# Seven PSUM banks in one tile, handed out one by one, in a fused attention and feed-forward kernel

## The chip, the cores and the metric

One Trainium2 chip, of which the kernel uses one core. The metric is the device time of one execution in microseconds. Five engines run their own instruction streams: TensorE (PE) multiplies matrices into PSUM, ScalarE (ACT) does exponentials and tanh, VectorE (DVE) does elementwise work, GpSimd (POOL) only sets constants at the start here, SyncE (SP) issues most DMAs. PSUM is used here as eight banks of 128 partitions x 512 float32 columns.

## The reference

The output mixes an attention block and a feed-forward block, token by token, with a sigmoid gate. There are 2048 tokens of 512 features, 32 heads of 16 features, and 1792 hidden features; everything is bf16.

```python
    def _A_ref(x, wqkv, wo):
        ...
        qkv = (lambda x, *d: x.transpose(*d))((x @ wqkv).reshape(B, S, 3, H, Dh), 2, 0, 3, 1, 4)
        q, k, v = qkv[0], qkv[1], qkv[2]
        scores = jnp.einsum("bhqd,bhkd->bhqk", q, k) * (Dh ** -0.5)
        p = _softmax(scores, axis=-1)
        o = jnp.einsum("bhqk,bhkd->bhqd", p, v)
        return (lambda x, *d: x.transpose(*d))(o, 0, 2, 1, 3).reshape(B, S, D) @ wo

    def _B_ref(x, w_gate, w_up, w_down):
        g = _silu(x @ w_gate)
        u = x @ w_up
        return (g * u) @ w_down

    x = A_x
    g = _sigmoid((x * gate_w).sum(-1, keepdims=True))
    a = _A_ref(x, A_wqkv, A_wo)
    b = _B_ref(x, B_w_gate, B_w_up, B_w_down)
    return g * a + (1 - g) * b
```

## The kernel before

**Tiling.** The attention is cut into 32 units: 4 blocks of 512 queries times 8 groups of 4 heads. Each unit walks over 16 key tiles of 128 keys. For one key tile of one unit there are 4 score blocks, one for each head, of 128 keys x 512 queries: one PSUM bank each. The 2048 score blocks are all computed by TensorE (`score`), with a contraction over 32 rows, so that up to four of them run side by side in the array.

**Two ways to an exponential.** Most score blocks go to ScalarE: `emit_pair` takes a PSUM tile of two banks from the pool `ps_s` (two such tiles in turn), puts two score blocks into it and lets ScalarE write the exponentials of 1024 columns to a tile `e_t` in SBUF, one of `EB` = 10. The other key tiles go to VectorE: `emit_d` puts one score block into a single bank, VectorE reads it with a multiply and an add into 16-bit integers (`c_t<-d_t` in the profile), and further VectorE instructions in SBUF (`copy`, or `bits` and `product`) make an exponential out of the bits. `v_unit`, `v_take` and `quad` choose which key tiles go that way and in which of the two forms. An `emit_d` rides along with the scores of a pair.

**PV.** `pv` multiplies the exponentials with the values and sums into one bank of its own (`ps_o`, tile `o_ps`), four column tiles of 32 at a time.

**Side work.** The projections (`kp`, `qp`, `vp`), the gated feed-forward (`gu`, `dps`) and the output projection (`ops`) are cut into pieces of four matmuls of 32 columns by `columns`. Each chain of pieces takes one bank from three single-bank pools `ps_m0` to `ps_m2` (`m_tile`), and VectorE or ScalarE reads the bank at its end (`m_free`). A `Pacer` releases chains by deadlines.

**The order.** Every instruction of an engine goes through a helper (lines 164, 167 and 176) that ties it to the one before on that engine, so the order in which the program is written is the order in which each engine runs. What decides it is a planner in Python, which keeps a running time for TensorE, ScalarE and VectorE (`plan.pe`, `plan.act`, `plan.dve`) and when each bank comes free (`banks`, and `s_end` for the two score tiles). The main loop fills the time until the next score tile is free with PV, side pieces or a short wait, and then emits the pair. Exponentials are collected in `exps` and written into the program by `flush_act` once the planner's time has reached them; VectorE's work is written by `fill_dve`. Which instruction waits for which is worked out by the framework from the tiles that they read and write.

```python
        def exp():
            act(out=e_t[:], in_=s_t[:], func=ACT.Exp, scale=inv_sqrt_dh)
            plan.act = max(plan.act, ready) + ACT_US
            s_end[i] = plan.act + SLOT
```

The start (transposing the input, the first keys, queries and values) and the end (the last rows of the output) are written out by hand; they use the same pools.

## Time and profile before

| what | value |
|---|---|
| median of 3 runs | 780.14 us (778.90 to 780.59) |
| the profiled execution: span from first to last instruction | 777.2 us |
| the profiled execution's own time | 777.15 us of span; what the runs add around it is 2.99 us to the median |
| ScalarE busy | 762.2 us in 861 instructions |
| TensorE busy | 741.1 us in 9412 matmuls |
| VectorE busy | 722.4 us in 1171 instructions |
| exponentials of two banks | 792, 743.8 us together, 1198 ns each |
| reads of single banks `d_t` by VectorE | 464 |
| mean granted TensorE clock | 0.999 of full speed |

The profile is of one execution. "Busy" is the time in which an engine had at least one instruction in it; since ScalarE overlaps instructions that follow each other, 792 instructions of 1198 ns take 743.8 us. Matmul ends are modelled. In the groups, the part after the bar is the busy time in us, the mean of one in ns, and the engine's idle time just before them with what ended it. A line of the waits reads: who waited, for whom, total us, how often, the longest.

### The profile page before, as it was taken

To read this page: it belongs to the slowest core of one execution; us is meant where nothing else is said; L and a number is where in the kernel's file an instruction comes from. 1 tells how busy PE (TensorE), PEld (TensorE's weight loads), DVE (VectorE), ACT (ScalarE), POOL (GpSimd) and SP (SyncE) were. 2 spreads that over 40 slices of the span, in tenths; PEclk is the share of its full clock that TensorE was granted. 3 is DMA by queue.
4 is the path that set the end of the run, shared out by engine and by line. 5 is a ranking of instruction groups with operands and counts; after the bars stand their busy time and mean duration, and the time that the engine had idled before them with its cause. 6 is when DMAs were issued, how large, how long until landed. Compare 5 with 4: busy or idle time off the path is not lost.

```text
span 777.2 us, 22732 instructions
## 1 busy us (share of the span) xinstructions
PE 741.1 (95%) x9412; PEld 237.2 (31%) x9413; DVE 722.4 (93%) x1171; ACT 762.2 (98%) x861; POOL 10.6 (1%) x25
## 2 busy tenths in 40 slices
PE   8999999999999999999999999999999989999997
PEld 3333333323332232333222233323322323333232
DVE  7799999999999999989999999999999899899992
ACT  6999999999999999999999999999999999999996
POOL 5000000000000000000000000000000000000000
PEclk9999999999999999999999999999999999999999
DMA  8002304144210112221100230311000322100001
GB/s 190 2 2 48 76 12 80 28 115 88 63 26 12 26 44 61 60 46 31 34 19 18 49 83 19 76 35 40 17 24 14 85 54 57 30 19 12 14 29 35
DMA packets 91022, 34.42 MB, mean 44 GB/s; under 512 B 75488, under 2 KB 90472, under 8 KB 90920
## 3 DMA queue, kind: packets, MB, share of 16 engines
q1 hardware_dynamic: 89192, 32.66, 17.5%
q8 instruction: 73, 1.20, 0.7%
q10 hardware_dynamic: 1728, 0.33, 0.2%
q14 instruction: 29, 0.24, 0.1%
HBM read 21.55 MB, written 2.35 MB: 31 GB/s over the span
## 4 chain that ended last, share of the span: by engine, by line
ACT 44%; PE 40%; issue 8%; DVE 7%; DMA 0%; ACTq 0%; DVEq 0%
ACT e_t L167 41%; PE s_t L164 15%; PE o_ps L164 10%; PE gu L164 7%; DVE c_t L176 5%; PE ops L164 4%; ACT th L167 4%; PE qp L164 1%; PE kp L164 1%; DVE kaug L176 1%; PE dps L164 1%; PE warm L164 1%; DVE mt L176 1%; DVE gs L176 0%; DMA wu<-in_B_w_up_dram 0%
## 5 line engine op out<-in xcount | busy, mean ns | idle before, releaser
L167 ACT ACTIVATE e_t<-s_t 128x1024 bf16<-128x1024 f32 x792 | 743.8, 1198 | 1.9 <-PE s_t L164 1.9
L176 DVE TENSOR_SCALAR c_t<-d_t 128x512 uint16<-128x512 f32 x404 | 268.7, 685 | 18.1 <-PE d_t L164 17.6
L164 PE MATMUL s_t<-qx,kaug 32*128 32x512 bf16 (+1 forms) x1248 | 243.5, 381 | 17.6 <-ACT e_t L167 14.5
L164 PEld LDWEIGHTS <-kaug 32*128 32x128 bf16 (+1 forms) x2048 | 103.8, 91 | 320.2 <-issue 314.8
L164 PE MATMUL o_ps<-e_t,vaug 128*32 128x512 bf16 (+3 forms) x1828 | 164.2, 356 | 0.0
L164 PE MATMUL d_t<-qx,kaug 32*128 32x512 bf16 x384 | 133.5, 384 | 0.0
L176 DVE TENSOR_SCALAR c_t<-c_t 128x2048 uint16<-128x2048 uint16 x187 | 125.7, 687 | 1.1
L164 PEld LDWEIGHTS <-vaug 128*32 128x32 bf16 x3416 | 74.9, 95 | 109.2 <-issue 89.3
L164 PE MATMUL o_ps<-c_t,vaug 128*32 128x512 bf16 (+3 forms) x1316 | 104.3, 334 | 1.0 <-DVE osb L176 0.5
L176 DVE TENSOR_TENSOR c_t<-c_t 128x2048 bf16<-128x2048 bf16 x63 | 76.7, 1218 | 0.0
L164 PE MATMUL gu<-xT,wg 128*32 128x512 bf16 x896 | 74.1, 384 | 0.0
L164 PE MATMUL gu<-xT,wu 128*32 128x512 bf16 x896 | 68.9, 382 | 0.0
L164 PE MATMUL ops<-wd_t,mt 128*32 128x512 bf16 x672 | 57.8, 382 | 0.0
L164 PE MATMUL s_t<-q,kaug 64*128 64x512 bf16 (+1 forms) x200 | 39.0, 382 | 7.5 <-ACT e_t L167 7.1
L167 ACT ACTIVATE th<-gu 128x512 bf16<-128x512 f32 x56 | 43.4, 775 | 0.0
L176 DVE SCALAR_TENSOR_TENSOR gs<-th,gu 128x512 bf16<-128x512 bf16 x56 | 38.2, 683 | 5.4 <-ACT th L167 5.2
L176 DVE SCALAR_TENSOR_TENSOR mt<-gs,gu 128x512 bf16<-128x512 bf16 x56 | 38.2, 682 | 1.5 <-PE gu L164 0.5
L176 DVE TENSOR_SCALAR kaug<-d_t 128x512 uint16<-128x512 f32 x56 | 37.4, 684 | 1.1 <-PE d_t L164 1.1
L164 PEld LDWEIGHTS <-mt 128*32 128x32 bf16 (+1 forms) x1037 | 23.6, 95 | 24.6 <-issue 21.3
L176 DVE TENSOR_SCALAR kaug<-c_t 128x2048 uint16<-128x2048 uint16 x39 | 26.8, 686 | 0.5 <-PE o_ps L164 0.4
L164 PEld LDWEIGHTS <-wu 128*32 128x32 bf16 x896 | 19.3, 95 | 22.8 <-issue 15.4
L164 PEld LDWEIGHTS <-wg 128*32 128x32 bf16 x896 | 16.2, 94 | 25.9 <-issue 25.4
(141 smaller groups left out, 436.3 us busy)
## 6 DMA issues: line engine op xcount, KB each, us to landing
wg<-in_B_w_gate_dram SPq DMA_DIRECT2D x56, 128.0 KB
wu<-in_B_w_up_dram SPq DMA_DIRECT2D x56, 128.0 KB
on<-osb SPq DMA_DIRECT2D x120, 16.0 KB
rb<-rr SPq DMA_DIRECT2D x15, 128.0 KB
wd_t<-in_B_w_down_dram SPq DMA_DIRECT2D x7, 256.0 KB
qx<-qst SPq DMA_DIRECT2D x96, 16.0 KB
qx<-aq SPq DMA_DIRECT2D x96, 16.0 KB
out_dram<-o_t SPq DMA_DIRECT2D x12, 128.0 KB
```

What stands on the lines that cost most here:

```text
L164: return ordered(nc.tensor.matmul(*args, **kw))
L167: ordered(nc.scalar.activation(*args, **kw))
L176: return lambda *a, **kw: ordered(f(*a, **kw))
```

## The change

The pools `ps_s` and `ps_m0` to `ps_m2` go. One tile `psum` of seven banks takes their place, and each bank is handed out by itself, to score blocks and side work alike (`take`, `single`, `runs`). `emit_group` replaces `emit_pair`: it takes one, two or three banks with a constant step (`choose`), which need not be neighbours, and one exponential reads them all in one instruction. The blocks are counted in quarters of a key tile, so that a group of three may straddle two key tiles. The ten tiles `e_t` become one tile `e_all` of 22 blocks. The planner's fixed delays are replaced by completion times: an exponential ends at its start plus 0.064 (or 0.167 after a wait) plus 0.4265 for each block, and so on.

```diff
-    etp = ctx.enter_context(tc.tile_pool(name="etp", bufs=EB))
+    etp = ctx.enter_context(tc.tile_pool(name="etp", bufs=1))
...
-    ps_s = ctx.enter_context(tc.tile_pool(name="ps_s", bufs=2, space=bass.MemoryType.PSUM))
+    ps_b = ctx.enter_context(tc.tile_pool(name="ps_b", bufs=1, space=bass.MemoryType.PSUM))
     ps_o = ctx.enter_context(tc.tile_pool(name="ps_o", bufs=1, space=bass.MemoryType.PSUM))
-    ps_m = [ctx.enter_context(tc.tile_pool(name=f"ps_m{i}", bufs=1, space=bass.MemoryType.PSUM)) for i in range(3)]
+    psum = ps_b.tile([P, NP, QBW], F32, name="psum")
...
-    banks = [0.0] * 3
-    held = [None] * 3
+    banks = [0.0] * NP
+    held = [None] * NP
+
+    FLIP, UNIT_US = 0.105, 0.217
+    TO_ACT, ACT_FIX, ACT_COL, ACT_IN = 0.485, 0.064, 0.4265, 0.167
+    ACT_PE, DVE_PE, PE_DVE, ACT_DVE = 0.055, 0.08, 0.24, 0.06
...
     def m_tile(name):
         while m_ready() is None:
             stuck()
-        i = min((i for i in range(3) if banks[i] is not None), key=lambda i: banks[i])
+        i = single()
         plan.pe = max(plan.pe, banks[i])
+        return take(i)
+
+    def take(i):
         banks[i] = None
-        held[i] = ps_m[i].tile([P, QBW], F32, tag=f"m{i}", name=name)
+        held[i] = psum[:, i, :]
         return held[i]
...
+    def runs(w, now):
+
+        ok = [b is not None and b <= now for b in banks]
+        return [(i, s) for s in range(1, NP) for i in range(NP - (w - 1) * s) if all(ok[i + k * s] for k in range(w))]
+
+    def single():
+
+        first = min(b for b in banks if b is not None)
+        now = max(first, plan.pe)
+        open_ = [i for i in range(NP) if banks[i] is not None and banks[i] <= now]
+        ...
+        return max(open_, key=lambda i: (left(i), -banks[i]))
...
-    def emit_pair(bs, ride=0):
-        i = pairs[0] % 2
-        plan.pe = max(plan.pe + (FLIP if plan.mode != "R" else 0.0), s_end[i])
+    e_all = etp.tile([P, NE, QBW], BF16, name="e_all")
+    def choose():
+
+        late = max(plan.pe, horizon() - LATEST)
+        ...
+        for w in range(most, 0, -1):
+            if best is not None and w < 2:
+                break
+            r = runs(w, late) or (runs(w, 1e9) if best is None and w <= 2 else [])
+            if not r:
+                continue
+            s = min(([i + k * d for k in range(w)] for i, d in r), key=spread)
+            ...
+            key = (n, bool(fit), w) if dry else (n > 0 or not want, w)
+            if best is None or key > best[0]:
+                best = key, s, n, got
+        return best and best[1:]
...
+    def emit_group(s, ride, rel):
+        nonlocal quarter, at_, begun
+        w = len(s)
+        bs = next_banks(w)
+        ...
+        k0, step = s[0], s[1] - s[0] if w > 1 else 1
+        s_t = psum[:, k0:k0 + (w - 1) * step + 1:step, :]
+        ...
         for k, b in enumerate(bs):
-            score(s_t[:, k * QBW:(k + 1) * QBW], b, 32 if ride else 64)
-            e_of[b] = e_t[:, k * QBW:(k + 1) * QBW]
-        for k in ride:
+            score(psum[:, s[k], :], b, 32 if riders or w != 2 else 64)
+            e_of[b] = e_all[:, e0 + k, :]
+            e_slot[b] = e0 + k
+        for k in riders:
             emit_d(k)
-        spend("R", 1)
+        spend("R", 2 if extra else 1)
         flush_act()
-        ready = plan.pe + 0.27
+        ready = start + TO_ACT
 
         def exp():
-            act(out=e_t[:], in_=s_t[:], func=ACT.Exp, scale=inv_sqrt_dh)
-            plan.act = max(plan.act, ready) + ACT_US
-            s_end[i] = plan.act + SLOT
+            act(out=e_all[:, e0:e0 + w, :], in_=s_t, func=ACT.Exp, scale=inv_sqrt_dh)
+            plan.act = max(plan.act + ACT_FIX, ready + ACT_IN) + ACT_COL * w
+            for i in s:
+                banks[i] = plan.act + ACT_PE
...
-    kp0 = ps_s.tile([P, 2 * QBW], F32, tag="s", name="kp0")
-    qp0 = m_tile("qp0")
+    def pair_at(i):
+        banks[i] = banks[i + 1] = None
+        return psum[:, i:i + 2, :].rearrange("p b q -> p (b q)")
+
+    kp0 = pair_at(0)
+    qp0 = take(4)
...
-        room = s_end[pairs[0] % 2] - plan.pe
+        s, ride, rel = s
+        room = max(rel, horizon() - LATEST) - FLIP - plan.pe
...
-        emit_pair([4 * n + 2 * half, 4 * n + 2 * half + 1], want_d())
-        half ^= 1
-        begun = 0
-        at_ += not half
-        forward()
+        emit_group(s, ride, rel)
```

More of the change, by code (lines that the diff above doesn't have):

```diff
@@ L116 @@
     EB = 10
+    NE = 22
+    NP = 7
     NY = 3
@@ L128 @@
     MUL_US = 1.135
+    LATEST = 0.64
     TINY = 1e-37
@@ L131 @@
     QLEAD = 24
-    SPARE = 0.5
+    SPARE = 0.3
     const = ctx.enter_context(tc.tile_pool(name="const", bufs=1))
@@ L305, in spend @@
         work_at.append((plan.pe, mms))
-        plan.pe = max(plan.pe + (FLIP if mode != plan.mode else 0.0), ready) + (0.226 if mode == "F" else 0.217) * mms
+        plan.pe = max(plan.pe + (FLIP if mode != plan.mode else 0.0), ready) + (0.226 if mode == "F" else UNIT_US) * mms
         plan.mode = mode
@@ L313, in later @@
             c.owed += 1
-        ready = plan.pe + 0.25 if ready is None else ready
+        ready = plan.pe + PE_DVE if ready is None else ready
         owed.insert(sum(o[0] <= ready for o in owed), (ready, cost, f, c, key))
@@ L358, in m_free, with left @@
         i = [h is ps for h in held].index(True)
-        banks[i], held[i] = t + 0.2, None
+        banks[i], held[i] = t + DVE_PE, None
+    def runs(w, now):
[5 more added lines that the diff above has]
+        open_ = [i for i in range(NP) if banks[i] is not None and banks[i] <= now]
+        def left(i):
+            keep, banks[i] = banks[i], None
+            n = len(runs(3, 1e9))
+            banks[i] = keep
+            return n
+        return max(open_, key=lambda i: (left(i), -banks[i]))
     def emit_piece(c):
@@ L604, in end @@
             vec.reciprocal(odds[:, :], ge[:, :])
-        later(0.5, end, plan.act + 0.2)
+        later(0.5, end, plan.act + ACT_DVE)
     def turn_odds():
@@ L623 @@
     FS = [(qb, fc) for qb in ORDER for fc in range(FC)]
-    w_gate, w_up, gs_of = {}, {}, {}
+    w_gate, w_up, gs_of, gs_at = {}, {}, {}, {}
     def w_load(i, gate):
@@ L642, in gate @@
             th = work.tile([P, QBW], BF16, tag="th", name="th")
-            flush_act(plan.pe + 0.4)
+            ready = plan.pe + TO_ACT - UNIT_US
+            flush_act(ready + 0.05)
             act(out=th[:], in_=gp[:, :], func=ACT.Tanh, scale=0.5)
-            plan.act = max(plan.act, plan.pe + 0.25) + 0.48
+            plan.act = max(plan.act + ACT_FIX, ready + ACT_IN) + ACT_COL
             def f():
@@ L651, in f @@
                 gs_of[i] = gs
-            later(0.6, f, plan.act + 0.25)
+            gs_at[i] = plan.act + ACT_DVE
+            later(0.62, f, gs_at[i])
         cs = slice(FS[i][0] * QBW, (FS[i][0] + 1) * QBW)
         return [columns(DC, "gu", lambda dc, w=w: w[i][:, dc, :], lambda dc: xT[:, dc, cs], end)
-                for w, end in ((w_gate, gate), (w_up, lambda p: later(0.6, lambda: gated(p))))]
+                for w, end in ((w_gate, gate), (w_up, lambda p: later(0.6, lambda: gated(p), max(plan.pe + PE_DVE, gs_at[i]))))]
     scaled = set()
@@ L690, in score @@
            tile_position=(r.start, 0))
-    FLIP = 0.107
-    SLOT = 0.28
-    s_end = [0.0, 0.0]
     e_end = {}
-    e_left = {}
-    pairs = [0]
-    def emit_pair(bs, ride=0):
-        i = pairs[0] % 2
-        plan.pe = max(plan.pe + (FLIP if plan.mode != "R" else 0.0), s_end[i])
-        plan.mode = "R"
-        ride = d_slots(1 - bs[0] % 4 // 2)[:ride]
-        s_t = ps_s.tile([P, 2 * QBW], F32, tag="s", name="s_t")
-        e_t = etp.tile([P, 2 * QBW], BF16, tag="e", name="e_t")
+    e_all = etp.tile([P, NE, QBW], BF16, name="e_all")
@@ new lines, with e_run, dur, horizon @@
+    e_slot = {}
+    e_next = [0]
+    def e_run(w):
+        used = set(e_slot.values())
+        for k in range(NE):
+            i = (e_next[0] + k) % NE
+            if i + w <= NE and not any(j in used for j in range(i, i + w)):
+                return i
+        return None
+    def dur(w):
+        return ACT_FIX + ACT_COL * w
+    def horizon():
+        return max(plan.act + dur(exps[-1][2]), exps[-1][0] + ACT_IN + ACT_COL * exps[-1][2]) if exps else plan.act
+    def fitting(w):
+        heads = {HEADS[b % 4] for b in next_banks(w)}
+        return [k for k in d_slots() if HEADS[k] not in heads]
@@ new lines, in choose, with spread @@
+    def choose():
+        late = max(plan.pe, horizon() - LATEST)
+        want = wants()
+        dry = thirst() < 1.5
+        side_b = int(side_bank())
+        most = min(3, 4 * (hi[au] - at_) - quarter) if au == UNITS - 1 else 3
+        def spread(s):
+            keep = [banks[i] for i in s]
+            for i in s:
+                banks[i] = None
+            left = len(runs(3, 1e9)) + len(runs(2, 1e9))
+            for i, t in zip(s, keep):
+                banks[i] = t
+            return max(max(keep), plan.pe), -left
+        best = None
+        for w in range(most, 0, -1):
[5 more added lines that the diff above has]
+            s = min(([i + k * d for k in range(w)] for i, d in r), key=spread)
+            rel = max(banks[i] for i in s)
+            others = sorted(b for i, b in enumerate(banks) if b is not None and i not in s and b <= max(late, rel))
+            n = max(0, min(want, len(others) - side_b, 3 - len(d_wait)))
+            fit = len(fitting(w)) if n else 0
+            n = min(n, fit) if fit or not dry else min(n, 1)
+            got = max(rel, others[n - 1]) if n else rel
+            key = (n, bool(fit), w) if dry else (n > 0 or not want, w)
+            if best is None or key > best[0]:
+                best = key, s, n, got
+        return best and best[1:]
@@ new lines, in next_banks @@
+    def next_banks(w):
+        r, a, t, q = [], au, at_, quarter
+        while len(r) < w and a < UNITS:
+            r.append(4 * (a * KT + t) + q)
+            q += 1
+            if q == 4:
+                q, t = 0, t + 1
+                while a < UNITS and t == hi[a]:
+                    a, t = a + 1, 0
+        return r
+    def emit_group(s, ride, rel):
+        nonlocal quarter, at_, begun
+        w = len(s)
+        bs = next_banks(w)
+        begun = 1
+        start = max(plan.pe + (FLIP if plan.mode != "R" else 0.0), rel)
+        spare[0] = min(spare[0] + max(0.0, horizon() - LATEST - start - 0.1), 1.5)
+        plan.pe = start
+        plan.mode = "R"
+        for i in s:
+            banks[i] = None
+        e0 = e_run(w)
+        e_next[0] = e0 + w
+        k0, step = s[0], s[1] - s[0] if w > 1 else 1
+        s_t = psum[:, k0:k0 + (w - 1) * step + 1:step, :]
+        riders = fitting(w)[:ride] if ride else []
+        extra = ride and not riders
+        if extra:
+            riders = d_slots()[:1]
@@ L715, in exp @@
         def exp():
-            act(out=e_t[:], in_=s_t[:], func=ACT.Exp, scale=inv_sqrt_dh)
-            plan.act = max(plan.act, ready) + ACT_US
-            s_end[i] = plan.act + SLOT
+            act(out=e_all[:, e0:e0 + w, :], in_=s_t, func=ACT.Exp, scale=inv_sqrt_dh)
+            plan.act = max(plan.act + ACT_FIX, ready + ACT_IN) + ACT_COL * w
+            for i in s:
+                banks[i] = plan.act + ACT_PE
             for b in bs:
-                e_end[b] = plan.act + 0.27
-        exps.append((ready, exp))
@@ L722, in emit_pair @@
-        for b in bs:
-            e_left[b] = pairs[0]
-        pairs[0] += 1
+                e_end[b] = plan.act + ACT_PE
+        exps.append((ready, exp, w))
+        for _ in bs:
+            quarter += 1
+            if quarter == 4:
+                quarter = 0
+                at_ += 1
+                begun = 0
+                forward()
+                begun = int(quarter > 0)
+            else:
+                begun = 1
+        begun = int(quarter > 0)
     exps = []
-    ACT_US = 0.905
@@ L729, in flush_act @@
     def flush_act(before=None):
-        while exps and (before is None or max(plan.act, exps[0][0]) <= before):
+        while exps and (before is None or max(plan.act - 0.33, exps[0][0]) <= before):
             exps.pop(0)[1]()
@@ L735, with d_slots @@
     y_live = [0]
-    def d_slots(half=None):
-        left = vcur["left"] if vcur else range(NV)
-        return [k for k in left if half is None or k // 2 == half]
+    def d_slots():
+        return list(vcur["left"] if vcur else range(NV))
     users = {}
@@ L797, in first @@
                     vops.append((0.6, lambda k=k: copy(n, k, h, y), ("y", n) if k == 1 else None, n, True))
-        d_wait.append((plan.pe + 0.5, first, n))
+        d_wait.append((plan.pe + UNIT_US + PE_DVE, first, n))
     waiting = {}
@@ L805, in ready @@
         copies[n, k] = (c.bitcast(BF16), h)
-        vready.append((plan.dve + 0.3, n, k))
+        vready.append((plan.dve + DVE_PE, n, k))
     def copy(n, k, i, y):
@@ L812, in copy @@
         if k == 3:
-            drop(i, plan.dve + 0.2)
+            drop(i, plan.dve + 0.05)
             y_live[0] -= 1
@@ L828, in product @@
         ready(n, 1, i, c)
-        drop(h, plan.dve + 0.2)
+        drop(h, plan.dve + 0.05)
         y_live[0] -= 1
@@ L884, in take_part @@
         vec.tensor_copy(out=o_part, in_=o_of[0][:, :])
-        o_end[0] = plan.dve + 0.2
+        o_end[0] = plan.dve + DVE_PE
         part_done.append(0)
@@ L927, in pv @@
                 e_of.pop(b)
-                e_left.pop(b, None)
+                e_slot.pop(b)
         pvs[un] += 1
         if un == 0 and pvs[0] == KT // 2:
-            later(0.6, take_part, plan.pe + 0.47)
+            later(0.6, take_part, plan.pe + UNIT_US + PE_DVE)
         spend("C", share, 0.0 if k is not None else max(e_end.pop(b, 0.0) for b in range(4 * n, 4 * n + 4)))
@@ L1038, in tail_ready @@
         assert here_done and len(scaled) == TQ
-        al = ps_s.tile([P, 2 * QBW], F32, tag="s", name="al")
-        a_ps.append(al)
+        a_ps.append(m_tile("al"))
     def tail(n):
@@ L1095 @@
     keep_warm(12)
-    tp = ps_s.tile([P, 2 * QBW], F32, tag="s", name="tp")
+    tp = pair_at(2)
     turn(DC - 1, [tp[:, 0:QBW], tp[:, QBW:2 * QBW]])
@@ L1099 @@
     pad(0)
-    tps = [m_tile("tp") for _ in range(2)]
+    tps = [take(i) for i in (5, 6)]
     turn(DC - 2, tps)
@@ L1127 @@
     plan.dve = plan.pe + 3.9
+    for i in range(4):
+        banks[i] = 0.0
     pace = Pacer()
@@ L1267 @@
     pace.add(last_pieces(), SLOTS - KT // 2, SLOTS, downs, cond=ripe)
-    au = at_ = half = begun = 0
+    au = at_ = quarter = begun = 0
     vu = 0
@@ L1313, in f @@
             post(un)
-            o_end[0] = plan.dve + 0.2
+            o_end[0] = plan.dve + DVE_PE
             finish(un)
@@ L1427 @@
     LEAD, LAST = 8.0, 6.0
-    TILE_US = 1.87
+    TILE_US = 1.82
     def forward():
         nonlocal au, at_
-        while au < UNITS and not half and not begun and at_ == hi[au]:
+        while au < UNITS and not begun and at_ == hi[au]:
             au, at_ = au + 1, 0
@@ L1442, in v_unit @@
                 return None
-            left = hi[vu] - (at_ + max(half, begun) if vu == au else 0)
+            left = hi[vu] - (at_ + begun if vu == au else 0)
             if vu >= au and left > 0 and (vu or hi[0] > KT // 2):
@@ L1461, in quad, with wants, thirst, side_bank @@
         if spare[0] > SPARE:
-            spare[0] = 0.0
+            spare[0] -= SPARE
             return False
         return True
-    def want_d():
-        if not vcur and v_unit() is None:
-            return 0
+    def wants():
+        if len(d_wait) >= 3 or not vcur and v_unit() is None:
+            return 0
+        return 2 if thirst() < 1.5 else 1
+    def thirst():
+        return 0.6 * len(d_wait) + sum(v[0] for v in vops) + plan.dve - plan.pe
+    def side_bank():
         c = pick()
-        one = c is not None and c.pieces[c.i][2] and (pace.credit > 0 or c.deadline <= plan.slot + 4)
-        open_ = sum(b is not None and b <= plan.pe for b in banks)
-        if not d_wait and len(vops) < 2:
-            one = False
-        return max(0, min(2, open_ - int(one), 3 - len(d_wait)))
+        return bool(c is not None and c.pieces[c.i][2] and (pace.credit > 0 or c.deadline <= plan.slot + 4)
+                and (d_wait or len(vops) >= 2))
     while au < UNITS:
@@ L1481 @@
         flush_act(plan.pe)
-        back = pairs[0] - min(e_left.values(), default=pairs[0])
-        if back >= EB - 1:
+        back = len(e_slot) // 2
+        if back >= EB or e_run(3) is None:
             next_pv()
             continue
-        room = s_end[pairs[0] % 2] - plan.pe
+        s = choose()
+        if s is None:
+            flush_act()
+            s = choose()
+            if s is None:
+                stuck()
+                continue
+        s, ride, rel = s
+        room = max(rel, horizon() - LATEST) - FLIP - plan.pe
         if room > 0.02:
@@ L1489 @@
             switch = 0.0 if plan.mode == "C" else FLIP
-            fits = int((room + SLACK - switch) / 0.216)
+            fits = int((room + SLACK - switch) / UNIT_US)
             c = side(room + SLACK)
@@ L1515 @@
                 spend("C", 1)
-                spare[0] += 0.22
                 continue
-            if room > 0.15:
+            if rel > plan.pe + 0.15:
                 plan.pe += 0.1
-                spare[0] += 0.1
                 continue
-        n = au * KT + at_
-        begun = 1
-        emit_pair([4 * n + 2 * half, 4 * n + 2 * half + 1], want_d())
-        half ^= 1
-        begun = 0
-        at_ += not half
-        forward()
+        emit_group(s, ride, rel)
     flush_act()
@@ L1568 @@
     tail(2)
-    rps = ps_s.tile([P, 2 * QBW], F32, tag="s", name="rps")
+    rps = m_tile("rps")
     spread_rows(rps, rt)
```

## The prediction

> **What bounds the kernel now.** I read the page's engine totals first, then the chain that ended last, then the costliest groups, the list of waits, and two stretches of the timeline for the price of single steps.

> ```profile
> PE 741.1 (95%) x9412; PEld 237.2 (31%) x9413; DVE 722.4 (93%) x1171; ACT 762.2 (98%) x861; POOL 10.6 (1%) x25
> ACT 44%; PE 40%; issue 8%; DVE 7%; DMA 0%; ACTq 0%; DVEq 0%
> L167 ACT ACTIVATE e_t<-s_t 128x1024 bf16<-128x1024 f32 x792 | 743.8, 1198 | 1.9 <-PE s_t L164 1.9
> L176 DVE TENSOR_SCALAR c_t<-d_t 128x512 uint16<-128x512 f32 x404 | 268.7, 685 | 18.1 <-PE d_t L164 17.6
> ```

> ScalarE (ACT) is busy 98% of a 777.2 us span, and 743.8 us of that are 792 exponentials, which follow each other every 743.8/792 = 0.939 us although one lasts 1.198: they overlap in the engine. TensorE (95%) and VectorE (93%) are nearly as full. The three run beside each other, and hardly wait:

> ```profile
> PE s_t L164 <- ACT e_t L167: 22.0, 73, 0.7
> DVE c_t L176 <- PE d_t L164: 17.6, 31, 1.5
> ACT e_t L167 <- PE s_t L164: 1.9, 5, 0.5
> ```

> Of 792 exponentials 5 found their scores late. So the time is the sum of 98% ScalarE work, and it stands only as long as each engine can work in one PSUM bank while the others work in theirs.

> **What the change does to ScalarE.** The built program of the changed kernel has 570 exponentials over two banks and 140 over three (1560 blocks of 512 columns; before 1584, since 488 blocks instead of 464 go to VectorE). At the pitch of the trace a pair is 0.939 us. A third block adds the difference of these two lone activations, 1.024 - 0.599 = 0.425:

> ```profile
> L167 ACT ACTIVATE xT<-tp 128x1024 bf16<-128x1024 f32 x1 | 1.0, 1024 | 0.5 <-PE tp L164 0.5
> L167 ACT ACTIVATE vaug<-vp 128x512 bf16<-128x512 f32 x1 | 0.6, 599 | 0.0
> ```

> 570 x 0.939 + 140 x 1.364 = 726.2 us, 17.6 less than 743.8. That is the whole gain on offer. VectorE's own sum hardly moves (24 more evictions at 0.665, 68 more copies at 0.67, 50 fewer products at 1.218: +1 us). TensorE gets 130 more sets of four PV matmuls at 0.215, +28 us.

> **What it does to the order.** Before, score pairs had a tile of their own with two buffers, the side work three more tiles. Now all seven banks are slices of one tile, `psum`. I listed both built programs with what each instruction waits for, and traced each wait to the instruction that meets it. Before, all 792 exponentials wait for their scores and for nothing of VectorE. After, 509 wait for a VectorE instruction, and it is always the last one that touched `psum`, of whatever bank. A stretch from the middle:

> ```
> VectorE  reads bank 5 (mt)          waits for the exponential of banks 2 and 4
> TensorE  scores into 1, 3 and 6     first waits for that VectorE read of bank 5
> VectorE  reads bank 0 (c_t)         waits for the score in bank 6
> ScalarE  exponential of 1 and 3     waits for that VectorE read of bank 0
> TensorE  score into bank 4          waits for that exponential of 1 and 3
> ```

> None of these waits joins two accesses of one bank. The recorded order treats the tile as one resource: whenever the engine that touches it changes, the new one waits until the last instruction of the old one is complete, reads after reads too. I call an unbroken run of one engine a turn. There are 2280 turns (ScalarE 738, VectorE 648, TensorE 894), and in 2272 of the 2279 changes the first instruction of the new turn waits for the last one of the old. So everything that touches the seven banks stands in one row, and the time is the sum of the turns, not the largest engine. Only the PV matmuls (they have the eighth bank) and VectorE's work in SBUF stay free to run beside it.

> **The sum.** ScalarE's turns cannot overlap with a neighbour, so a lone exponential costs what it lasts: the fastest of the 792 took 1.017 us, as the lone xT copy did (1.024). 543 turns of a pair x 1.02 = 553.9. 136 of a triple x (1.02 + 0.42) = 195.8. 29 of a tanh and a pair x (0.60 + 0.94) = 44.7, 4 of a tanh and a triple x 1.96 = 7.8, 26 others of 512 columns x 0.60 = 15.6. Together 817.8 us.

> VectorE's turns hold 709 reads of the tile: 662 of 512 columns x 0.685 (the row above) = 453.5, 16 pairs of a value eviction and its column of the gate at 0.615 + 0.152 = 12.3, and some 6 us of small ones: 472 us.

> TensorE's turns: the last set of up to four matmuls that run together lasts 0.39, and each set ahead of it adds 0.215. These lines of the timeline have three sets and one:

> ```profile
> 299.63 0.82 PE L164 MATMUL gu<-xT,wu 128*32 128x512 bf16 x12
> 303.34 0.40 PE L164 MATMUL gu<-xT,wg 128*32 128x512 bf16 x4
> ```

> A switch between scores and column tiles adds 0.11 to 0.14 (a score at 301.19, the next set at 301.51, 0.32 instead of 0.215); I take 0.12. The 894 turns hold 894 last sets, 900 others (104 of them PV sets that stand between two accesses) and 689 switches: 348.7 + 193.5 + 82.7 = 625 us.

> Each change costs the way from an end to the next start. The tail of the trace is such a row already:

> ```profile
> 768.90 0.61 PE L164 MATMUL o_ps<-e_t,vaug 128*32 128x512 bf16 x8
> 769.57 0.69 ACT L167 ACTIVATE osb<-o_ps,tiny 128x512 bf16<-128x512 f32 x1 [0.54 <-PE o_ps L164]
> 770.31 0.25 PE L164 MATMUL dt<-sel_t,osb 128*128 128x4 bf16 x4 [0.26 <-ACT osb L167]
> 770.60 0.26 DVE L176 RECIPROCAL rt<-dt 128x16 bf16<-128x16 f32 x1 [1.83 <-PE dt L164]
> 770.95 0.41 PE L164 MATMUL rps<-ident,rt 128*32 128x128 bf16 x16
> 771.48 0.88 DVE L176 TENSOR_TENSOR on_l<-osb,rps 128x128 bf16<-128x128 bf16 x4 [0.62 <-PE rps L164]
> ```

> From end to start: 769.51 to 769.57, 770.26 to 770.31, 770.56 to 770.60, 770.86 to 770.95, 771.36 to 771.48, so 0.04 to 0.12. I take 0.06, which the first three are nearest to: 2279 x 0.06 = 137 us.

> What stays outside the row is covered: between two turns of TensorE lie 1.54 us of other engines' turns on average, against 0.14 us of PV matmuls queued there (124 us over 894), and VectorE has 186 us of other work against over 1400 us of foreign turns; laid against each other gap by gap, only 6 of VectorE's pieces stick out, by 1 us in all. Without that cover the two would add up to 310 us. DMA has more time per step than before; the edits of waits and thresholds inside the planner have their whole effect in the order counted here.

> 818 + 472 + 625 + 137 = 2052. The first access of the tile comes after 5.6 us, the first turns wait 1 us for loads, after the last access the output takes 3.2 us (773.9 to 777.2), and the profiled execution lies 3.0 under the median of the runs (777.15 against 780.14): 2052 + 5.6 + 1 + 3.2 + 3.0 = **2064.8 us**, 2.6 times the time before. The ends: hand-overs of 0.03 or 0.13 give -68 or +160; exponentials as long as in the full stream (1.20) instead of 1.02 give +128; evictions at their fastest (0.627) -38.

> **Rivals.** *The waits cost nothing, and it gets faster.* The planner counts on bank-by-bank use, and the waits join different banks, so if the chip were found already past them, ScalarE would fall by 17.6 us. TensorE, at 741 + 28 = 769, would then be the longest, and the time about 768. This decides if the turns overlap by over 1280 of the 2052 us. For it: before, the same engines did overlap. Against it: an instruction that waits for a completion cannot overlap with it, and 2272 changes are of that sort. Chance 0.05. [...]

> *Part of the row dissolves.* Should long PV stretches or loads set the pace in some stages while other stages overlap, some 1200 to 1930 us. I see nothing for it but the 7 free changes. Chance 0.06.

> *TensorE's clock falls.* It works 36% of the time instead of 95%. At half clock its turns would cost up to 625 us more, 2690; if the clock is low half of the time, 2380. The end of the trace shows how long it holds:

> ```profile
> 773.00:774.00 1.00, 0.00 (x0) 0.00 (x0) 0.77 (x2) 0.84 (x2) 0.00 (x0) 1.00 0.00 0
> 775.00:776.00 1.00, 0.00 (x0) 0.00 (x0) 0.00 (x0) 0.00 (x0) 0.00 (x0) 1.00 0.73 255
> 776.00:777.20 1.20, 0.00 (x0) 0.00 (x0) 0.00 (x0) 0.00 (x0) 0.00 (x0) 0.51 0.00 0
> ```

> The last matmul ends at 772.97 and the granted clock (third column from the right) is 1.00 until 776: three idle microseconds are forgiven. Of the 893 gaps between TensorE's turns 12 are longer than that, so I expect full clock almost throughout. Chance 0.14. [...]

> That the change does not do what it says is excluded by the list of exponentials.

> **How the numbers follow.** The full row at full clock has 0.75. Its own range, 1930 to 2350, takes in the bounds above (not all at once at the upper end) and the milder third of the clock case, and so holds about 0.8. Runs of this kernel can be told apart at about 0.2%. Slower has the row, its dissolving and the clock, 0.94 with rounding; faster is the first rival, 0.05; 0.01 for no change.

> **What would show it.** Right: ScalarE's share falls from 98% to about 40%, TensorE and VectorE to about 35%; the waits are led by TensorE on ScalarE (some 600 times), VectorE on TensorE, ScalarE on VectorE, hundreds each; the chain has ScalarE near 40%, TensorE 30%, VectorE 23%; exponentials last 1.02 and 1.44 us. Wrong: ScalarE still over 90% busy, or under 200 such waits; a granted clock below 0.9 would mean the third rival, hand-overs above 0.1 us the upper end.

## The result, and the profile after

The changed kernel takes **2454.93 us** (median; 2453.96 to 2456.78) against 780.03 us before: a ratio of **3.148** (95% interval 3.144 to 3.153). The forecast was 2064.8 us. The direction and the row of turns came true. The clock did not, and the time was missed by 390 us.

The page's engine totals and the shares of the chain that ended last, of the changed kernel:

```profile
PE 1354.6 (55%) x10093; PEld 332.3 (14%) x10093; DVE 770.8 (31%) x1213; ACT 824.9 (34%) x779; POOL 10.6 (0%) x25
PEclk6555555555555555555555555555555555555556
PE 41%; ACT 33%; DVE 20%; issue 5%; SPq 1%; DVEq 0%; DMA 0%; ACTq 0%
```

ScalarE is busy a third of the time instead of 98%. The busy shares of the three engines, 55, 31 and 34%, now add up to 120%, where before they added up to 286%: the engines take turns, and only PV work and VectorE's work in SBUF run beside them. The middle line is the clock that TensorE was granted, in 40 slices: 5 tenths almost throughout, where every slice of before showed 9 (that is, 90% or more):

```profile
PEclk9999999999999999999999999999999999999999
```

The list of waits of the changed kernel, longest first, without TensorE's weight loads:

```profile
DVE c_t L179 <- PE psum L167: 792.1, 325, 7.1
PE psum L167 <- ACT e_all L170: 785.6, 589, 3.9
ACT e_all L170 <- PE psum L167: 655.6, 329, 5.1
ACT e_all L170 <- DVE c_t L179: 623.6, 247, 4.6
PE psum L167 <- DVE c_t L179: 158.8, 152, 2.6
```

The wait of TensorE for an exponential was 22.0 us in 73 times; now it is 785.6 us in 589. ScalarE waited for TensorE 5 times; now 329 times, and 247 times for a VectorE read of a score block, a wait that did not exist. A stretch of the timeline shows the row itself (start, duration, engine, operation; in brackets the idle time before it and what ended it). Only rows of the tile `psum` are shown; PV, weight loads and VectorE's work in SBUF run between them:

```profile
1000.71 0.62 PE L167 MATMUL psum<-xT,wg 128*32 128x512 bf16 x4
1001.44 1.45 ACT L170 ACTIVATE e_all<-psum 128x1536 bf16<-128x1536 f32 x1 [1.87 <-PE psum L167]
1002.94 1.04 PE L167 MATMUL psum<-xT,wg 128*32 128x512 bf16 x8 [1.61 <-ACT e_all L170]
1004.03 0.60 ACT L170 ACTIVATE th<-psum 128x512 bf16<-128x512 f32 x1 [1.14 <-PE psum L167]
...
1005.20 1.04 PE L167 MATMUL psum<-qx,kaug 32*128 32x512 bf16 x6
1006.35 1.02 ACT L170 ACTIVATE e_all<-psum 128x1024 bf16<-128x1024 f32 x1 [1.72 <-PE psum L167]
1007.40 0.69 DVE L179 TENSOR_SCALAR c_t<-psum 128x512 uint16<-128x512 f32 x1 [6.49 <-ACT e_all L170]
```

On each side of the dots, a line begins 0.03 to 0.11 us after the end of the one before: the feed-forward matmuls end at 1001.33 and the exponential of three banks starts at 1001.44, it ends at 1002.89 and the next feed-forward matmuls start at 1002.94, though they go on with a chain in another bank. At the dots TensorE is still in PV matmuls when the tanh ends (1004.63), and its scores begin 0.57 us later. But a set of four matmuls lasts 0.62 here, not 0.39, and two sets 1.04, not 0.60.

ScalarE's groups, shapes kept apart (last figure before the second bar: mean of one in ns):

```profile
L170 ACT ACTIVATE e_all<-psum 128x1024 bf16<-128x1024 f32 x570 | 583.8, 1024 | 1312.0 <-PE psum L167 540.3 <-DVE c_t L179 540.3 <-DVE kaug L179 71.5
L170 ACT ACTIVATE e_all<-psum 128x1536 bf16<-128x1536 f32 x140 | 203.1, 1451 | 260.0 <-PE psum L167 115.3 <-DVE c_t L179 83.3 <-DVE mt L179 16.1
```

### The profile page after: what moved, and what is told of

Same layout as the page of the kernel before. It is cut to its first block, busy times and chain, and to the rows that moved or that the text cites. A ratio compares the mean times of both kernels' runs of the same rounds, so it can differ in the third digit from the quotient of the medians.

```text
span 2453.7 us, 24073 instructions
## 1 busy us (share of the span) xinstructions
PE 1354.6 (55%) x10093; PEld 332.3 (14%) x10093; DVE 770.8 (31%) x1213; ACT 824.9 (34%) x779; POOL 10.6 (0%) x25
## 4 chain that ended last, share of the span: by engine, by line
PE 41%; ACT 33%; DVE 20%; issue 5%; SPq 1%; DVEq 0%; DMA 0%; ACTq 0%
PE psum L167 39%; ACT e_all L170 32%; DVE c_t L179 12%; DVE kaug L179 2%; DVE mt L179 2%; PE o_ps L167 2%; DVE gs L179 2%; ACT th L170 1%; SPq L179 1%; DVE qst L179 1%; DVE o_t L179 0%; DVE vaug L179 0%; DVEq L179 0%; DVE on L179 0%; ACTq L170 0%
## 5 line engine op out<-in xcount | busy, mean ns | idle before, releaser
L170 ACT ACTIVATE e_all<-psum 128x1024 bf16<-128x1024 f32 (+1 forms) x710 | 786.9, 1108 | 1572.0 <-PE psum L167 655.6
L179 DVE TENSOR_SCALAR c_t<-psum 128x512 uint16<-128x512 f32 x416 | 286.8, 691 | 977.8 <-PE psum L167 792.1
L167 PE MATMUL psum<-qx,kaug 32*128 32x512 bf16 (+1 forms) x1632 | 367.0, 592 | 363.8 <-ACT e_all L170 229.5
L167 PE MATMUL o_ps<-e_all,vaug 128*32 128x512 bf16 (+3 forms) x1964 | 256.2, 526 | 1.2 <-ACT e_all L170 1.2
L167 PEld LDWEIGHTS <-kaug 32*128 32x128 bf16 (+1 forms) x2048 | 111.7, 99 | 876.5 <-issue 875.3
L167 PE MATMUL o_ps<-c_t,vaug 128*32 128x512 bf16 (+3 forms) x1780 | 220.4, 539 | 1.5 <-DVE c_t L179 1.4
L167 PE MATMUL psum<-wd_t,mt 128*32 128x512 bf16 x896 | 131.1, 610 | 146.6 <-ACT e_all L170 126.7
L167 PE MATMUL psum<-xT,wu 128*32 128x512 bf16 x896 | 128.3, 600 | 150.9 <-ACT e_all L170 94.8
L167 PE MATMUL psum<-xT,wg 128*32 128x512 bf16 x896 | 130.7, 607 | 145.6 <-ACT e_all L170 132.6
L167 PEld LDWEIGHTS <-vaug 128*32 128x32 bf16 x4096 | 114.9, 117 | 218.9 <-issue 216.7
L167 PE MATMUL psum<-xT,wqk 128*32 128x512 bf16 x512 | 73.9, 600 | 82.5 <-ACT e_all L170 64.9
L167 PE MATMUL psum<-q,kaug 32*128 32x512 bf16 (+1 forms) x256 | 74.7, 594 | 60.1 <-ACT e_all L170 31.9
L167 PEld LDWEIGHTS <-mt 128*32 128x32 bf16 (+1 forms) x1037 | 40.1, 109 | 265.0 <-issue 260.9
L167 PEld LDWEIGHTS <-wu 128*32 128x32 bf16 x896 | 30.9, 106 | 248.0 <-issue 247.6
L167 PE MATMUL psum<-rb,xT 128*32 128x449 bf16 (+1 forms) x320 | 38.2, 496 | 44.3 <-ACT e_all L170 34.7
L167 PEld LDWEIGHTS <-wg 128*32 128x32 bf16 x896 | 29.5, 106 | 234.6 <-issue 233.7
L167 PE MATMUL psum<-wo_t,on 128*32 128x512 bf16 (+2 forms) x207 | 30.7, 588 | 35.8 <-ACT e_all L170 30.3
L167 PE MATMUL psum<-on,kaug 32*128 32x512 bf16 (+1 forms) x128 | 32.9, 590 | 30.7 <-ACT e_all L170 23.0
```

Of the source, the lines that this page charges most:

```text
L167: return ordered(nc.tensor.matmul(*args, **kw))
L170: ordered(nc.scalar.activation(*args, **kw))
L179: return lambda *a, **kw: ordered(f(*a, **kw))
```

## The experiments

Two theories went into them. **A:** the loss is the row of turns through the one tile, and the 390 us above the forecast are TensorE's half clock in it. **B:** the new order itself, with triples that straddle key tiles, is slow.

**One part alone: the tile.** The kernel before with its five PSUM tiles made slices of one; pairs, planner and order untouched.

```diff
-    ps_s = ctx.enter_context(tc.tile_pool(name="ps_s", bufs=2, space=bass.MemoryType.PSUM))
-    ps_m = [ctx.enter_context(tc.tile_pool(name=f"ps_m{i}", bufs=1, space=bass.MemoryType.PSUM)) for i in range(3)]
+    ps_b = ctx.enter_context(tc.tile_pool(name="ps_b", bufs=1, space=bass.MemoryType.PSUM))
+    psum = ps_b.tile([P, 7, QBW], F32, name="psum")   # score pairs: banks 0-1 and 2-3; side work: 4 to 6
```

Expected: 

> The kernel before, where only the two score buffers and the three single banks become slices of one PSUM tile of seven banks; planner, pairs and order as before. In the built program 2496 turns stand in a row (ScalarE 800, VectorE 625 with 685 reads, TensorE 1071 with 1905 sets and 612 switches). Theory A: by the same sum with TensorE at half clock (last set 0.61, each set ahead 0.43): 841 + 456 + 1085 + 150 + 13 = 2545 us; at full clock it would be 2130. Rival B (triples, straddling or the new planner are the cause): about 780 us.

Measured (one execution): 2545.7 us, clock 0.507. The sum gave 2545. From its waits:

```profile
ACT e_t L173 <- PE psum L170: 1101.8, 528, 4.1
PE psum L170 <- ACT e_t L173: 799.1, 658, 3.4
```

So B is out: without a triple, a straddle or the new planner, the tile alone costs 1766 us, and the sum of turns at half clock holds for another order too. That it holds to a microsecond is luck: TensorE's turns took 27 us less and the hand-overs 26 us more than the sum has (the table below).

**The waits undone.** The changed kernel, where each access of the tile is declared independent of all others except those of its own banks (and those that share data elsewhere).

```diff
+            tc.declare_no_dep(ins.ins, group="banks", keep=keep, reason="other banks")
+            tc.add_to_no_dep_group("banks", ins.ins)
...
-            return lambda *a, **kw: ordered(f(*a, **kw))
+            return lambda *a, **kw: own_banks(ordered(f(*a, **kw)), "DVE", a, kw)
```

In the first version (the run e_free) the order is that of the changed kernel, and an exponential waits for all banks from its lowest to its highest. Expected: 

> The changed kernel in its own order of instructions, but an access of the PSUM tile waits only for accesses of the banks that it spans, from its lowest to its highest (so an exponential over banks 0 and 6 still waits for those between; 197 such waits of exponentials are left, of 1000). Theory A (the row of waits is the loss): 780 to 860 us, the 197 waits at up to 0.4 us each on top of 770, clock 0.99. Rival B (the new order itself is slow): above 1500 us.

Measured: 999.49 us, a ratio of 1.282 (1.278 to 1.286) to before, clock 0.89. Over 1450 us are gone with the waits, so the row is shown. But the time is far above the 780 to 860 us expected: exponentials waited 144.5 us for TensorE, 188 times, and the clock fell in part again. How much of this comes from the 197 waits left, and how much from the clock, was not separated. Exponentials over banks that are not neighbours, with waits for exactly their banks, were not tried, and what they would give is left open.

In the second version (e_contig) a group's banks are neighbours, which also changes the order:

```diff
-        return [(i, s) for s in range(1, NP) for i in range(NP - (w - 1) * s) if all(ok[i + k * s] for k in range(w))]
+        return [(i, s) for s in (1,) for i in range(NP - (w - 1) * s) if all(ok[i + k * s] for k in range(w))]
```

Expected: 

> The changed kernel with two edits: an access of the one PSUM tile waits only for accesses of its own banks (the others are declared free of a dependency), and a group of banks must be neighbours (step 1). 707 exponentials (555 pairs, 151 triples). Theory A (the loss is the row of waits between different banks, at half of TensorE's clock): the row is gone, so ScalarE's 762 - 744 + 727 = 745 us and TensorE's 741 + 27 = 768 us bound it, 765 to 800 us, granted clock 0.99. Rival B (the planner's new order or the triples cost the time themselves): above 1500 us. Rival C (the waits are gone, but the declared waits sit late or the order has holes without the row): 850 to 1200 us.

Measured: 796.99 us, a ratio of 1.0225 (1.0197 to 1.0252), clock 0.99. The row is gone, and yet the change is no gain. Three of its longer waits name two reasons:

```profile
PEld L223 <- DVE kaug L235: 25.8, 34, 1.4
ACT e_all L226 <- PE psum L223: 19.5, 42, 3.7
PE psum L223 <- DVE kaug L235: 11.7, 31, 1.0
```

The first and third are waits that my own declaration left standing. The longest of the second (3.7 us) is at the start, where the new order begins with a key projection whose weights are still on their way (a weight load waits 2.7 us for the DMA of `wqk`).

Without the waits on `kaug` (e_contig2: where two instructions touch different parts of the key tile, they are now told apart even if one takes it as integers and the other as bf16), expected: 

> The kernel of the run e_contig, but scores no longer wait for VectorE writes to another part of the key tile (there a copy in 16-bit integers and the bf16 keys were taken as overlapping; 34 weight loads waited 25.8 us for it, and matmuls 11.7 us). Theory A (these waits and the start are what keeps it above before): 797 less most of 37 us, 765 to 780 us. Rival E (the bank-wise order has no gain to give: exponentials take 0.967 and 1.460 us each from start to start, because their scores come just in time): 785 to 797 us.

Measured: 783.88 us, 1.0046 (1.0029 to 1.0063). Then the start as well, and fewer waits (e_contig4):

```diff
-                    prev = [pace.add(k_pieces(b, tb), 0, d - 40 + tb, prev)]
+                    prev = [pace.add(k_pieces(b, tb), 2, d - 40 + tb, prev)]
...
+            if engine == "PE":
+                by_bank[b].clear()
```

Expected: 

> The kernel of the run e_contig2, with the pieces of the key projection held back to the third step (in e_contig TensorE stood 2.4 us and ScalarE 3.7 us at the start, waiting for their weights), and without waits that a matmul into the same bank has already served. 548 pairs and 153 triples. Theory A: 4 us less than e_contig2, 760 to 776 us. Rival E: 780 to 793 us.

Measured: 778.55 us, 0.9974 (0.9964 to 0.9984). Both runs landed between A and E. The first edit was worth 13.1 us. The second was worth 5.3 us, but it also moved the order: by the traces ScalarE does 1552 blocks instead of 1564. This version is 0.3% faster than before.

**Where the gain of the triples went.** Groups of two at most (e_pairs):

```diff
-        most = min(3, 4 * (hi[au] - at_) - quarter) if au == UNITS - 1 else 3
+        most = min(2, 4 * (hi[au] - at_) - quarter) if au == UNITS - 1 else 2
```

Expected: 

> The kernel of the run e_contig4 with groups of two banks at most, so 776 pairs and no triples; bank-wise waits as there. Theory T (triples bring the gain that the change was made for: a start saved for each third block, 0.965 x 3 / 2 - 1.467 = -0.02, so nothing at the pitch measured in e_contig4): 775 to 783 us. Rival U (triples save 0.06 us of ScalarE each and keep three banks moving): 785 to 800 us.

Measured: **772.47 us**, 0.9907 (0.9892 to 0.9921): the fastest version, 0.9% faster than before and faster than with triples. Theory T was right that triples bring nothing, but the time lies 2.5 us below its 775 to 783. The totals of the run e_contig4 (first line) and of e_pairs:

```profile
PE 739.4 (95%) x10093; PEld 248.3 (32%) x10093; DVE 729.7 (94%) x1227; ACT 750.1 (97%) x769; POOL 10.6 (1%) x25
```
```profile
PE 742.5 (96%) x9984; PEld 245.0 (32%) x9985; DVE 739.4 (96%) x1234; ACT 751.6 (97%) x843; POOL 10.6 (1%) x25
```

ScalarE works 1.5 us less with triples (for four blocks more), and it idles 26.7 us of its span of 776.8 with them, 19.4 of 771.0 without. Why it idles more with them was not separated, since the order differs too. The figure of 1.467 us for a triple in my expectations was misread: in a kernel with two shapes, the time in which a triple overlaps a pair stands in both groups. The expectations of e_contig4, of e_pairs and of the two runs below count two pairs too many (each trace has two other instructions of 1024 columns). The traces have 546 pairs, 153 triples and one single, 1552 blocks, for e_contig4 and 774 pairs, 1548 blocks, for e_pairs. From the engine's total, less the 18.4 us that ScalarE spends on other work before (762.2 - 743.8), a block costs 0.4696 us before, 0.4715 with triples and 0.4736 with pairs alone. A triple saves 0.02 us, not the 0.04 that the two lone activations gave.

Of the 17.6 us that the change was to save ScalarE, 11.3 were blocks sent to VectorE (24 at 0.4696), and only 6.2 were the triples. In e_contig4 ScalarE's work did fall by 12.1 us (762.2 to 750.1): 32 blocks fewer make 15.0, and the dearer blocks take 3 of them back. Its idle time rose from 15.0 to 26.7 us, which used up the rest.

Then the time by which scores run ahead of ScalarE, `LATEST`, was changed from 0.64 in e_contig4 to 0.80 and 0.50. Expected of the first: 

> The kernel of the run e_contig4 with scores written up to 0.80 us before ScalarE runs dry, instead of 0.64; 571 pairs, 144 triples. Theory V (in e_contig4 exponentials cost 0.965 and 1.467 from start to start, against 0.939 for a pair before, since their scores come too late for the start to overlap): the pitch of a pair falls to 0.93 to 0.95, that of a triple to 1.40, 571 x 0.94 + 144 x 1.40 = 738 us; time 768 to 777 us. Rival W (a bank held longer is a bank missing elsewhere): 779 to 790 us.

Measured: 782.92 us, 1.0045 (1.0029 to 1.0062), in rival W's range. The totals give 0.4695 us a block, so starts overlap again as V said (a pair lasts 1.118 us on average, and two blocks cost 0.939), but the planner sends 1572 blocks to ScalarE instead of 1552. ScalarE works 6.4 us more and idles 3.3 us less. Whether a want of banks moved the blocks, as W has it, is not shown.

Expected of the second: 

> The kernel of the run e_contig4 with 0.50 us instead of 0.64, the other way; 532 pairs and 153 triples, 28 blocks more on VectorE. Theory V: the overlap goes altogether, 1.02 for a pair and 1.45 for a triple, with idle time between, 785 to 800 us. Rival W: 770 to 778 us.

Measured: 796.86 us, 1.0225 (1.0209 to 1.0242), in V's range. The overlap went only in part: a block costs 0.488 us, between the 0.4696 of before and the 0.512 of a lone pair. The idle time of ScalarE rose to 32.2 us. Of the three leads tried, 0.64 us is the best for triples, and all three are slower than pairs alone at 0.64; pairs alone at other leads were not run.

**The clock.** The changed kernel, with its row and its order, and extra matmuls by zero weights (fillers) in TensorE's idle time. Each of these four runs (fill4, fill2, fill6, fillv) is one execution:

```diff
             act(out=e_all[:, e0:e0 + w, :], in_=s_t, func=ACT.Exp, scale=inv_sqrt_dh)
+            if closed in o_of and 0 < pvs[closed] and pv_left(closed) > 1 and (closed or pvs[0] != KT // 2):
+                for _ in range(4):
+                    for j in range(4):
+                        mm(o_of[closed][32 * j:32 * j + 16, :], lhsT=vaug[:, 0, G * 4 * VC:], rhs=xT[:, 0, 0:QBW],
+                           start=False, stop=False, tile_position=(0, 32 * j), skip_group_check=True)
```

Expected of four sets: 

> The changed kernel with four extra sets of PV-like matmuls by zero weights (they add zero to the open PV sum) written behind nearly every exponential, where TensorE waits for it. The row of turns is the same. Theory A (the 390 us above the forecast are TensorE's half clock, which falls because TensorE works too small a share of the time): the clock comes back to over 0.95, and the time falls to about the forecast of 2065 us, or up to 2200 where the fillers stick out. Rival D (hand-overs and single steps are dearer than forecast, the clock does not matter or cannot be held): 2450 us or more; at half clock four sets last 1.7 us and stick out of an exponential's 1.02 by 0.7, 2900 us.

Measured: 2177.27 us, clock 0.893; theory A's time, but not its clock.

```profile
PE 1479.9 (68%) x19612; PEld 537.9 (25%) x19613; DVE 770.8 (35%) x1213; ACT 824.2 (38%) x779; POOL 10.6 (0%) x25
PEclk8998799988998898988898978899889999998889
```

Adding 9520 matmuls (16 behind each of 595 exponentials) made the kernel 278 us **faster**. The forecast of 2065 plus the 21% of the time at half clock (0.21 x 390 = 83) is 2148; 29 us are left for fillers that stick out. The turns, added up from the trace, agree: ScalarE's and VectorE's are the same to 1 us, TensorE's fall from 987.5 to 686.5 us, and the hand-overs, in which fillers that stick out are counted, rise from 162.1 to 186.3.

Two sets, expected: 

> As fill4, with two extra sets behind an exponential instead of four. Theory F (the clock follows the share of time in which TensorE works, over a few us): between the 0.52 without fillers and the 0.89 with four, 0.60 to 0.75; each tenth of clock is worth 78 us of the 390, so 2065 + 390 x 2 x (1 - clock) = 2260 to 2380 us. Rival G (only idle stretches of over 3 us lower the clock): two sets close no such stretch that four did not close, so 0.89 and about 2150 us.

Measured: 2335.37 us, clock 0.683; theory F gives 2065 + 390 x 0.63 = 2312. Rival G, a loss only by long idle stretches, is out: TensorE idled for over 3 us once with two sets (3.03 us) and never with four, and the clock is 0.2 lower.

Six sets, expected: 

> As fill4, with six extra sets. Theory F: clock 0.97 to 1.00. The row is then the forecast's 2065 us, and six sets with two switches (1.5 us) stick out of an exponential's 1.02 (with a VectorE turn behind it, not): by 0.4 us in about half of the 738 turns, 2065 + 150 = 2215 us. If the clock stays at 0.89 the cause of its fall is not the share of work: 2300 us.

Measured: 2188.74 us, clock 0.916: within 27 us of F's time, but with a lower clock than F said. The time is near by luck: the hand-overs grew by 57 us to 219.4, not by the 150 that F had for fillers that stick out, and that makes up for the clock. And fillers behind VectorE's reads too, expected: 

> As fill4 (four extra sets behind an exponential), and three more behind each VectorE read of a score block. The row of 2280 turns is the same. Theory F (the clock follows the share of time in which TensorE works): clock 0.96 or more, and the time comes to the forecast's 2065 us plus what sticks out (three sets and two switches are 0.9 us against 0.69 of the read, where TensorE is next: 268 times 0.2): 2100 to 2160 us. Rival H (the clock has come back already as far as it matters, and the rest of fill4's 2177 us is fillers that stick out): 2200 us or more.

Measured: 2179.99 us, clock 0.911: F's clock and time were both missed, and H's 2200 us too. Full clock throughout was reached in no run with the row (the highest mean was fill6's 0.916): where no PV sum is open (some 16% of the exponentials) the fillers have no place to go, and 29 of the 33 falls of the clock in fillv's trace come after a stretch of 3.4 us without any filler. So the row at full clock from end to end was not measured; 2065 us for it is an estimate. A straight line through TensorE's turns and the clock of the changed kernel and of each filler run leads to 595 to 611 us of turns at full clock (an estimate), near the forecast's 625.

## Why the prediction was wrong

The traces allow the sum to be checked term by term. A turn is taken from the first start to the last end of an unbroken run of one engine's instructions that touch `psum`, and a hand-over from there to the next start. (Ends of matmuls are modelled, so the border between TensorE's turns and the hand-overs behind them is less sure than their sum.)

| us | forecast | changed kernel | onetile, expected | onetile |
|---|---|---|---|---|
| ScalarE's turns | 818 | 820.8 | 841 | 842.7 |
| VectorE's turns | 472 | 473.9 | 456 | 457.4 |
| TensorE's turns | 625 | 987.5 | 1085 | 1058.1 |
| hand-overs | 137 | 162.1 | 150 | 176.2 |
| the ends, and what the runs add | 12.8 | 10.7 | 13 | 11.2 |

- **The row of turns: right.** The trace of the changed kernel has the 2280 turns of the forecast (894, 738 and 648), that of onetile the 2496 of its expectation, and in neither does a turn start before the one ahead of it has ended.
- **ScalarE's and VectorE's terms: right**, to 3 and 2 us. An exponential takes 1.024 or 1.451 us for 1.02 or 1.44, a read 0.691 for 0.685.
- **Hand-overs: 25 us too low.** One takes 0.071 us on average instead of 0.06: about 0.1 behind TensorE, 0.03 to 0.06 behind the others, and some are longer, as at the dots above.
- **TensorE's term: wrong, by 362 of the 390 us.** The durations put in were those of a busy engine at full clock. With those of the changed kernel's trace, 0.61 for a last set and 0.43 for one ahead of it, the same counts give 894 x 0.61 + 900 x 0.43 + 689 x 0.12 = 1015 us, and 2064.8 + 390 = 2455. That this meets the 2454.93 measured is luck: 1015 is 27 us above the turns of the trace, and the hand-overs make up for it.
- **The step that failed** is the reading of the tail in the clock rival: "three idle microseconds are forgiven", and from it "full clock almost throughout", with a chance of 0.14 for the other case. Idle stretches of over 3 us were indeed rare: in the changed kernel TensorE has one (3.88 us). The clock was at half in 690 of 717 stretches of 3.4 us all the same, and the mean was 0.519, which the prediction had named as the sign of this rival. The tail shows one fall of the clock, at 776.03, and not what brought it about; and the 3.4 us before it were not idle throughout, since the last matmul ends 0.35 us into them. So the reading was too strong. The rival's price was also too high: all of TensorE's turns were doubled, but a last set at half clock lasts 0.61 us, not 0.78.
- **The first rival** (waits undone, about 768 us) is only in part tested. With neighbouring banks and without the row, other orders took 772 to 797 us; the changed kernel's own order, with 197 waits left, took 999. Its reason is not borne out: TensorE, with 131 more sets of PV in e_contig4 than before, counted by columns, was busy 739.4 us and not 769. Why the 28 us for them do not show is open.

## What to carry to other kernels

Ask of every shared tile what the framework takes as one resource. Before pools are merged, list which instruction each access waits for; a wait between two different banks is the sign. Where engines take turns, price each step alone (an exponential of two banks took 1.024 us here, where the full stream had one every 0.939), and do not take for granted the clock that TensorE had when it was full (here 0.999 before, and 0.519 in the changed kernel, where it was busy 55% of the span). Zero-weight matmuls in its idle time can then be worth more than they cost: in fill4 the kernel was 278 us faster with them.

## What the hardware showed

```profile
200.78:204.19 3.41, 1.49 (x10) 0.31 (x7) 0.69 (x1) 1.02 (x1) 0.00 (x0) 0.50 0.00 0
204.19:207.60 3.41, 3.33 (x33) 0.99 (x34) 2.09 (x4) 1.45 (x1) 0.00 (x0) 0.51 0.00 0
207.60:211.02 3.42, 1.43 (x27) 0.60 (x20) 1.60 (x4) 1.15 (x2) 0.00 (x0) 0.99 0.00 0
211.02:214.43 3.41, 1.32 (x11) 0.34 (x11) 1.00 (x3) 1.19 (x2) 0.00 (x0) 0.50 0.00 0
```

After a stretch in which TensorE worked 98% at half clock comes one at full clock. In that one TensorE works 42% and never idles longer than 1.65 us, and the next is at half clock again.

Four runs (the changed kernel, fill2, fill4, e_free), cut into such stretches from the first instruction to the last, give these counts:

- At full clock, 208 stretches were followed by half clock. Their busy shares were 0.12 to 0.67, with medians of 0.41 to 0.52 by run. None was idle throughout; the longest time without a matmul in any of them is 2.87 us. The 795 that were followed by full clock had 0.45 or more.
- At half clock, the 207 stretches that were followed by full clock had 0.80 or more, with medians of 0.92 to 1.00. But 98 stretches with 0.80 or more were followed by half clock, so the share of work alone does not account for the changes.

The counts do not show what sets the clock. By the forecast's counts a row at full clock would have TensorE at work 36% of the time (an estimate: 749 of 2065 us), less than any of the 795 stretches had. In the changed kernel TensorE was busy 55% of the span, and 22 stretches at half clock were followed by full clock, which mostly lasted for one stretch.
